# 64-row tile products, val by blocks one group earlier, tangent features on VectorE, and a new order, in a cosformer and SwiGLU kernel

## The chip, the cores and the metric

The kernel runs on one core of a Trainium2 chip. A core has TensorE (PE: matrix products, with weight loads that overlap them), VectorE (DVE), ScalarE (ACT), GpSimd (POOL) and SyncE (SP); POOL and SP issue most of the DMAs. Work data lie in SBUF, products land in the eight banks of PSUM. The metric is the time of one execution on the device in microseconds (us), the median over runs.

## The reference

Two layers behind one another: an attention without softmax, linear in the sequence, and a gated feed-forward block.

```python
batch, n_heads, seq, head_dim = (8, 8, 576, 64)
theta = np.pi / 2.0 * np.arange(S) / S
def phi(x, c, s):                       # c, s: cos and sin of theta
    r = np.maximum(x, 0.0)
    return np.concatenate([r * c, r * s], axis=-1)
q_p, k_p = phi(q, cos_w, sin_w), phi(k, cos_w, sin_w)
kv = np.einsum('bhsf,bhsd->bhfd', k_p, v)
z = np.sum(k_p, axis=2)
num = np.einsum('bhsf,bhfd->bhsd', q_p, kv)
den = np.einsum('bhsf,bhf->bhs', q_p, z)[..., None] + 1e-06
x = (num / den).transpose(0, 2, 1, 3).reshape(B * S, H * D)      # 4608 x 512
g, val = x @ w_gate, x @ w_val                                   # 512 x 1536 each
out = (g * (1.0 / (1.0 + np.exp(-g))) * val) @ w_out             # 1536 x 512
```

The kernel divides the features by the cosine: a query row then has the features relu(q) and relu(q) times its tangent.

## The kernel before, in words

**Tiles and groups.** The 4608 tokens are 36 tiles of 128, four tiles to a group, nine groups (0 to 8). A tile is two slots of 64 tokens; a batch is nine slots, so tile 4 has a slot of batch 0 and one of batch 1, tiles 5 to 8 lie in batch 1, and so on.

**Attention.** For each batch the key sums `kv` and `z` come from `kv_job` (line 716): 64-row, 64-column products in the four quarters of PE's array. For batches from 2 on the query features are written to `r_q` (`feature_jobs`): relu by VectorE in two instructions, and nine instructions that multiply a slot by its tangent and take the relu, on ScalarE (line 877; batch 7 does both kinds on ScalarE, line 867). A DMA transpose on SP's queue turns them to `phit` (line 839). A tile's products with the key sums are in `tile_jobs`: line 785 for tiles of batches from 2 on, line 779 for tiles 4 to 8. The latter multiply 128 rows, two heads one above the other, with a block-diagonal matrix (`kvd`, `kvd1`) of 130 columns: eight products a tile, sixteen in tile 4. Then come the denominator (line 797), its reciprocal (line 803), the product with it into `x` (line 807), and the turn of `x` to `xT`: by PE for tiles 4 to 7 (line 755), by a DMA transpose on SP's queue from tile 8 on (line 747).

**Feed-forward.** A group has twelve slices of 128 hidden columns, in three units u = 0, 1, 2 of four slices. Gate and val of a unit can be taken in two ways. Plain: four slices of four products of 512 columns each (`plain_fc`, line 904, or `plain_val`, line 1052). By blocks (`block_jobs`, line 977): seven products of sums instead of eight, each of four matmuls of 256 columns; VectorE makes sums of `xT` (line 950), of the weights (line 499), and two adds for each unit between the products (lines 997 and 1005 or 1013), ScalarE copies two products (line 628). `GATE_FROM` and `VAL_FROM` say from which (group, unit) on blocks are used: gate from (1, 0), val from (2, 1). The multiplication of silu(gate) with val is line 1061 (plain) or line 1072 (blocks). The output projection is plain in group 0 (line 1262) and by blocks from group 1 on (line 1142), behind token sums by VectorE (line 1093).

**Loads.** `batch_loads` puts a `hold_job` ahead of loads on GpSimd's queue: a tiny copy that reads a given tile, so that what is queued behind it starts only when that tile is there. Batch 3's k and v and batch 4's q are held by tile 8's `xT`.

**The order.** The first quarter of group 0 follows a list written out by hand (`words`). Everything behind it is a set of `Job`s, each with engines, a duration, what it comes after, and rooms (banks, buffers) it takes and gives back; `order_once` plays them through on these costs and due times, shaken by a list of `SEEDS`, one for each `WINDOW` of planned time, and the instructions are emitted by planned start.

Of the kernel before, what the change touches and what calls it, by code (L numbers as in the profile page):

```python
# [19 lines left out]
def kernel(  # L20
# [10 lines left out]
    nc = tc.nc  # L31
# [374 lines left out]

    xT = {}
# [175 lines left out]
    TAIL = {"PE": 206.0, "ACT": 160.0, "DVE": 140.0, "POOL": 150.0, "SP": 150.0}  # L583
    PAD = 12.0
# [19 lines left out]
    def sc(n, sbuf=False):  # L604
        return 69 + n / 1.2 + (27 if sbuf else 0) + PAD

# [29 lines left out]
    def relu_on(eng, out, in_):  # L636
# [11 lines left out]
    LOADED = {("k", 1): 440.0, ("v0", 1): 7580.0, ("v1", 1): 9080.0, ("sa", 1): 10080.0, ("sb", 1): 14480.0, ("q", 2): 22280.0,  # L648
              ("k", 2): 25580.0, ("v", 2): 29580.0, ("q", 3): 32380.0}
    WO_AT = ((0, 2, 11330.0), (2, 4, 12580.0), (4, 8, 16980.0), (8, 12, 19480.0))  # L650
    W_AT = {8: (1750.0, 3060.0), 10: (4820.0, 6130.0)}
# [19 lines left out]
    DEN_ON = {"ACT": 100}  # L671
# [35 lines left out]
    def kv_job(b, key, after):  # L707
# [12 lines left out]
        mm = pe(1404, fn, key, after=after, get=[r], chore=b > 1)  # L720
        outs = []
        for n in range(2):
            for i in range(2):
# [8 lines left out]
                outs.append(Job({"ACT": 402, "DVE": 450} if b == 1 else {"ACT": 402}, fn, after=[mm] + J_.get(("tiles", b - 2), []), put=[r]))  # L732
# [11 lines left out]
    def turn_job(t, x, after, by_pe=False, key=None):  # L744
        if not by_pe:
            def fn(j):
                nc.sync.dma_start_transpose(out=xT_of(t), in_=one(x_all, x))
            J_["xT", t] = Job({"SP": 1450}, fn, after=after + J_.get(("xT_read", t // OUT - 3), []), put=[x], tail=X_LAND, dma=(1430.0, X_SVC))
# [7 lines left out]
        mm = pe(230, fn, key, after=after, get=[r], put=[x])  # L756
# [5 lines left out]
    X_LAND = 4000.0  # L762
    X_SVC = 1030.0
    PHI_LAND = 11500.0

    def tile_jobs(t, key, by_pe=False):
# [3 lines left out]
        def fn(j):  # L770
            ps = bank(r)
            for e in range(2):
                for g in range(G):
                    for ms, b, c, n in parts_of(t):
                        if b < 2:
                            if g % 2:
                                continue
                            for w in range(2):
                                nc.tensor.matmul(  # L779
                                    out=ps[ms, e, g * D1:(g + 2) * D1],  # L780
                                    lhsT=late[:, 2 * (t % 2) + w, e, g // 2].rearrange("p c s -> p (c s)")[:, ms],
                                    rhs=(kvd1 if b else kvd)[:, e, g // 2, w].rearrange("p i x -> p (i x)"),
                                    start=w == 0, stop=w == 1)
                            continue
# [4 lines left out]
        mm = pe(690 if 0 in bs else 455 if 1 in bs else 520 if len(bs) == 2 else 262, fn, key, after=sum((J_["kv", b] + turned_for(b, t) for b in bs), []), get=[r, one_at], chore=not by_pe)  # L789

        def view():
            return bank(r)[:, :, 0:2 * J * D1].rearrange("p e (y x) -> p e y x", x=D1)

        def fn(j):
            o, i_ = den_all[:, t % 4].rearrange("p (e y) o -> p e y o", e=2), view()[:, :, :, D:D1]
# [8 lines left out]
        rec = Job({"DVE": 132}, fn, after=[den])  # L804

        def fn(j):
            tt(out=one(x_all, x).rearrange("p (y e d) -> p e y d", e=2, d=D), in0=view()[:, :, :, 0:D],  # L807
               in1=rec_all[:, t % 4].rearrange("p (e y) o -> p e y o", e=2).to_broadcast([P, 2, 4, D]), op=ALU.mult)
# [8 lines left out]
    def load_job(b, nm, after, lands, behind):  # L817
        def fn(j):
            (load_turned if nm == "q" else load)(b, nm)
        J_["load", b, nm] = Job({"POOL": 1600 if nm == "q" else 780}, fn, after=after, tail=lands, behind=behind, dma=(1940.0, 2460.0) if nm == "q" else (470.0, 3770.0))  # L820

    def hold_job(read, after, put=()):
        def fn(j):
            nc.gpsimd.tensor_copy(out=hold2, in_=read())
        jb = Job({"POOL": 480}, fn, after=after, put=put)
# [3 lines left out]
    def batch_jobs(b, key):  # L829
# [11 lines left out]
        turned = [Job({"SP": 7500}, fn, after=phis + J_.get(("tiles", b - 2), []), tail=PHI_LAND - 7500, dma=(7600.0, 1370.0))]  # L841
# [10 lines left out]
    def feature_jobs(b):  # L852
# [10 lines left out]
        if b in PHI_ACT:  # L863
            for c in range(NC):
                for w in range(2):
# [3 lines left out]
                    phis.append(Job({"ACT": 412}, fn, after=loaded_q + before + J_["tanq"], rel=landed))  # L869
        else:  # L870
# [4 lines left out]
            for c in range(NC):  # L875
                def fn(j, c=c):
                    nc.scalar.activation(out=home()[:, :, c, 1], in_=raws[b, "q"][:, :, c], func=AF.Relu,  # L877
                                         scale=tanq[:, c:c + 1])
                phis.append(Job({"ACT": 430}, fn, after=loaded_q + before + J_["tanq"], rel=landed))
# [81 lines left out]
    def block_jobs(tg, u, which, order):  # L961
# [10 lines left out]
        def product(r, a, x, first, key, after, **kw):  # L972
# [6 lines left out]
            return pe(437.6, fn, key, after=after, **kw)  # L979
# [125 lines left out]
    def store_jobs(t, after, put, queues, cols=slice(0, d_model)):  # L1105
        for e in range(2):
# [6 lines left out]
            Job({q_: 560}, fn, after=after, put=put, tail=6500.0, dma=(1270.0, 480.0))  # L1113
# [9 lines left out]
    def out_jobs(tg, key):  # L1123
# [10 lines left out]
        def product(n, rs, a, b, first, after, get=(), parts=((range(HC), (0, 1)),), keys=()):  # L1134

            res = []
            for m, (kcs, its) in enumerate(parts):
# [7 lines left out]
                res.append(pe(len(kcs) * len(its) * 109.4, fn, at, after=after(kcs, its), behind=res, get=get if not m else ()))  # L1145
# [151 lines left out]
    def turned_tiles(ts, key):  # L1297
# [14 lines left out]
        mm = pe(200 + 236 * len(ts), fn, key, after=[], get=[r], rel=LOADED["sa" if ts[-1] < 6 else "sb", 1])  # L1312
# [57 lines left out]
    VAL_FROM = (2, 1)  # L1370
# [309 lines left out]
```

## Time and profile before

| | us |
|---|---|
| median of three runs | 298.43 |
| lowest, highest | 298.17, 299.18 |
| the profiled execution, first to last instruction (span) | 296.4 |
| busy: PE, VectorE, ScalarE, GpSimd | 291.1, 252.0, 199.4, 69.6 |

The profile is of one execution; its own time is known as the span, and what lies around the span is in the runs' times alone. PE's clock was granted in full from the first slice to the last. Line numbers are those of the kernel before. In the views that follow, a group reads: line, engine, operation, what is written from what, shapes, count, then busy us, mean ns of one, idle us just ahead, and what ended that idle time.

### The profile page before, as it was taken

To read this page: it belongs to the slowest core of one execution; us is meant where nothing else is said; L and a number is where in the kernel's file an instruction comes from. 1 tells how busy PE (TensorE), PEld (TensorE's weight loads), DVE (VectorE), ACT (ScalarE), POOL (GpSimd) and SP (SyncE) were. 2 spreads that over 40 slices of the span, in tenths; PEclk is the share of its full clock that TensorE was granted. 3 is DMA by queue.
4 is the path that set the end of the run, shared out by engine and by line. 5 is a ranking of instruction groups with operands and counts; after the bars stand their busy time and mean duration, and the time that the engine had idled before them with its cause. 6 is when DMAs were issued, how large, how long until landed. Compare 5 with 4: busy or idle time off the path is not lost.

```text
span 296.4 us, 8073 instructions
## 1 busy us (share of the span) xinstructions
PE 291.1 (98%) x3244; PEld 238.7 (81%) x3244; DVE 252.0 (85%) x514; ACT 199.4 (67%) x421; POOL 69.6 (23%) x122
## 2 busy tenths in 40 slices
PE   8999999999999999999999999999999999999994
PEld 4597465776787888898898889888988888888883
DVE  7878997879877999999988987998679868986883
ACT  6564346989559968985699589967465556565630
POOL 7963630003007012221352023200220050002000
PEclk9999999999999999999999999999999999999999
DMA  7999999997989997799996979940470046002026
GB/s 266 225 196 198 202 206 207 203 205 121 194 177 144 229 190 122 151 171 149 174 203 133 186 113 162 183 81 2 107 110 2 0 97 119 2 0 73 0 58 157
DMA packets 71973, 40.89 MB, mean 138 GB/s; under 512 B 48768, under 2 KB 68736, under 8 KB 71936
## 3 DMA queue, kind: packets, MB, share of 16 engines
q0 software_dynamic: 24800, 24.39, 49.1%
q1 hardware_dynamic: 46528, 15.47, 28.9%
q10 hardware_dynamic: 608, 0.52, 0.7%
q8 instruction: 25, 0.41, 0.6%
q14 instruction: 12, 0.10, 0.1%
HBM read 37.75 MB, written 9.44 MB: 159 GB/s over the span
## 4 chain that ended last, share of the span: by engine, by line
PE 97%; DVE 1%; issue 0%
PE banks L977 45%; PE banks L1142 24%; PE banks L1052 5%; PE banks L1262 4%; PE banks L438 4%; PE banks L904 4%; PE banks L187 3%; PE banks L716 3%; PE banks L785 2%; PE banks L779 1%; PE banks L372 1%; PE banks L1310 0%; PE banks L315 0%; PE banks L418 0%; PE banks L351 0%
## 5 line engine op out<-in xcount | busy, mean ns | idle before, releaser
L1111 POOL DMA_DIRECT2D out_dram<-ob x52 | 27.3, 532 | 104.8 <-ACT ob L630 69.7
L1036 ACT ACTIVATE sg<-banks 128x512 bf16<-128x512 f32 x72 | 41.3, 599 | 5.6 <-PE banks L977 5.4
L977 PEld LDWEIGHTS <-wg_sb 128*128 128x128 f16 x384 | 36.9, 98 | 6.3
L628 ACT COPY banks<-banks 128x512 f32<-128x512 f32 (+1 forms) x53 | 29.9, 572 | 17.5 <-PE banks L977 7.3
L1142 PEld LDWEIGHTS <-ht 128*128 128x128 f16 x384 | 37.4, 98 | 4.8
L1072 DVE TENSOR_TENSOR ht<-sg,banks 128x512 f16<-128x512 bf16 x60 | 39.9, 680 | 0.9 <-PE banks L977 0.6
L977 PEld LDWEIGHTS <-wgs_sb 128*128 128x128 f16 x368 | 35.7, 98 | 4.6
L997 DVE TENSOR_TENSOR banks<-m,banks 128x512 f32<-128x512 f32 x44 | 30.2, 693 | 10.6 <-ACT m L628 8.1
L977 PEld LDWEIGHTS <-wv_sb 128*128 128x128 f16 x320 | 31.0, 98 | 3.8
L977 PE MATMUL banks<-kvt,wgs_sb 128*128 128x256 f16 x236 | 33.4, 273 | 0.0
L1142 PEld LDWEIGHTS <-sums 128*128 128x128 f16 x288 | 27.9, 98 | 3.3
L630 ACT ACTIVATE ob<-banks 128x512 f32<-128x512 f32 x32 | 18.8, 596 | 15.9 <-PE banks L1142 15.2
L977 PE MATMUL banks<-xT,wg_sb 128*128 128x256 f16 x192 | 28.8, 273 | 0.0
L628 ACT COPY m<-banks 128x512 f32<-128x512 f32 x44 | 25.5, 590 | 4.4 <-PE banks L977 4.3
L1142 PE MATMUL banks<-wo_sb,ht 128*128 128x256 f16 x192 | 25.7, 273 | 0.0
L1142 PE MATMUL banks<-wt_sb,sums 128*128 128x256 f16 x192 | 24.9, 273 | 0.0
L977 PE MATMUL banks<-xT,wv_sb 128*128 128x256 f16 x160 | 24.0, 273 | 0.0
L1036 ACT ACTIVATE sg<-m 128x512 bf16<-128x512 f32 x24 | 15.1, 630 | 12.4 <-DVE m L1005 12.2
L807 DVE TENSOR_TENSOR x<-banks,rec 128x512 f16<-128x512 f32 x32 | 21.6, 686 | 1.5 <-DVE rec L803 0.2
L977 PE MATMUL banks<-kvt,wg_sb 128*128 128x256 f16 x168 | 22.4, 273 | 0.0
L1142 PE MATMUL banks<-wt_sb,ht 128*128 128x256 f16 x192 | 22.3, 273 | 0.0
L877 ACT ACTIVATE r_q<-raw_q,tanq 128x256 bf16<-128x256 bf16 x45 | 20.7, 510 | 0.1
(160 smaller groups left out, 544.7 us busy)
## 6 DMA issues: line engine op xcount, KB each, us to landing
out_dram<-ob POOLq DMA_DIRECT2D x52, 128.0 KB, 3.9
raw_kv<-in_k_dram POOLq DMA_DIRECT2D x7, 576.0 KB, 5.9
raw_q<-in_q_dram POOLq DMA_DIRECT2D x12, 288.0 KB, 10.7
raw_kv<-in_v_dram POOLq DMA_DIRECT2D x6, 576.0 KB, 8.3
out_dram<-ob SPq DMA_DIRECT2D x12, 128.0 KB, 2.5
wg_sb<-in_moe_w_gate_dram POOLq DMA_DIRECT2D x5, 256.0 KB, 8.9
wv_sb<-in_moe_w_val_dram POOLq DMA_DIRECT2D x5, 256.0 KB, 9.5
wo_sb<-in_v_dram SPq DMA_DIRECT2D x2, 576.0 KB, 4.2
```

The source lines that it names most:

```text
L438: nc.tensor.matmul(out=st["f", tg, fc, lo][i], lhsT=(wg_sb, wv_sb)[i][:, kc, fs], rhs=xT[tg][:, ts, kc], start=(kc == 0), stop=(kc == KC - 1))
L628: nc.scalar.copy(out=out, in_=in_)
L630: nc.scalar.mul(out=out, in_=in_, mul=mul)
L807: tt(out=one(x_all, x).rearrange("p (y e d) -> p e y d", e=2, d=D), in0=view()[:, :, :, 0:D], in1=rec_all[:, t % 4].rearrange("p (e y) o - ...
L877: nc.scalar.activation(out=home()[:, :, c, 1], in_=raws[b, "q"][:, :, c], func=AF.Relu, scale=tanq[:, c:c + 1])
L977: nc.tensor.matmul(out=to[:, i], lhsT=a[:, c, 2 * u + i], rhs=x()[:, :, c], start=first and i == 0 and c == 0, stop=c == KH - 1, skip_grou ...
L997: tt(out=bank(c), in0=one(m7_all, m).rearrange("p i x -> p (i x)"), in1=bank(b), op=ALU.add)
L1036: nc.scalar.activation(out=gates(rooms[w])[:, :, jh * HT:(jh + 1) * HT], in_=src, func=AF.Silu, scale=DOWN)
L1052: nc.tensor.matmul(out=bank(v), lhsT=wv_sb[:, kc, fc * P:(fc + 1) * P], rhs=xT[tg][:, :, kc], start=(kc == 0), stop=(kc == KC - 1))
L1072: tt(out=ht[:, 4 * u + w:4 * u + w + 3:2, jh * HT:(jh + 1) * HT], in0=gates(rooms[w])[:, :, jh * HT:(jh + 1) * HT], in1=src.rearrange("p ( ...
L1111: {"POOL": nc.gpsimd, "SP": nc.sync, "ACT": nc.scalar}[j.eng].dma_start(out=out_v[idx // NC, idx % NC][:, cols], in_=ob_of(t)[e * SH:(e + ...
L1142: nc.tensor.matmul(out=to, lhsT=a[:, kc, i * P:(i + 1) * P], rhs=b[:, kc], start=first and kc == 0 and i == 0, stop=kc == HC - 1, skip_gro ...
```

## The change

Five things, and with them the whole order of the jobs behind the hand-written list.

```diff
 tile_jobs, tiles of batches 0 and 1
-                            if g % 2:
-                                continue
                             for w in range(2):
-                                nc.tensor.matmul(
-                                    out=ps[ms, e, g * D1:(g + 2) * D1],
-                                    lhsT=late[:, 2 * (t % 2) + w, e, g // 2].rearrange("p c s -> p (c s)")[:, ms],
-                                    rhs=(kvd1 if b else kvd)[:, e, g // 2, w].rearrange("p i x -> p (i x)"),
-                                    start=w == 0, stop=w == 1)
+                                for i in range(0 if g % 2 else 2):
+                                    rows = slice(i * D, (i + 1) * D)
+                                    nc.tensor.matmul(
+                                        out=ps[ms, i, (g + e) * D1:(g + e + 1) * D1],
+                                        lhsT=late[rows, 2 * (t % 2) + w, e, g // 2].rearrange("p c s -> p (c s)")[:, ms],
+                                        rhs=(kvd1 if b else kvd)[rows, e, g // 2, w, i], start=w == 0, stop=w == 1)
...
-        mm = pe(690 if 0 in bs else 455 if 1 in bs else 520 if len(bs) == 2 else 262, fn, key, ...)
+        mm = pe(386 if 0 in bs else 352 if 1 in bs else 387 if len(bs) == 2 else 259, fn, key, ...)
...
+            x_, rec_ = one(x_all, x), heads(rec_all[:, t % 4])
+            if pairs and not by_pe:
+                for jj in range(J):
+                    ys = slice(2 * jj, 2 * jj + 2)
+                    tt(out=x_.rearrange("p (j i e d) -> p j i e d", i=2, e=2, d=D)[:, jj], in0=view()[:, :, ys, 0:D],
+                       in1=rec_[:, :, ys].to_broadcast([P, 2, 2, D]), op=ALU.mult)
+                return
 turn_job, by PE
-                nc.tensor.transpose(out=ps[:, kc], in_=one(x_all, x)[:, kc * P:(kc + 1) * P], identity=ident16)
+                nc.tensor.transpose(out=ps[:, kc], in_=one(x_all, x)[:, by_pairs(kc) * P:(by_pairs(kc) + 1) * P], identity=ident16)
 feature_jobs, batches 2 to 6
-                    nc.scalar.activation(out=home()[:, :, c, 1], in_=raws[b, "q"][:, :, c], func=AF.Relu,
-                                         scale=tanq[:, c:c + 1])
-                phis.append(Job({"ACT": 430}, fn, after=loaded_q + before + J_["tanq"], rel=landed))
+                    nc.vector.tensor_scalar(out=home()[:, :, c, 1], in0=raws[b, "q"][:, :, c], scalar1=tanq[:, c:c + 1],
+                                            scalar2=0.0, op0=ALU.mult, op1=ALU.max)
+                phis.append(Job({"DVE": 197}, fn, after=loaded_q + before + J_["tanq"], rel=landed))
 val by blocks
-    VAL_FROM = (2, 1)
+    VAL_FROM = (1, 0)
 batch 3's loads
-            if b == 3:
-                batch_loads(lambda: xT[2][0:1, 0, 0, 0:2], [J_["xT", 8]], names)
-            else:
+            if b > 3:
                 batch_loads(phit_read, J_["turned", b - 1], names)
         for t, s in tiles:
             tile_jobs(t, (tg, s / 4))
+            if t == 11:
+                batch_loads(lambda: xT[2][0:1, 3, 0, 0:2], [J_["xT", 11]], names)
 the planner's costs and the order
-    PAD = 12.0
+    PAD = 1.0
...
-        mm = pe(1404, fn, key, after=after, get=[r], chore=b > 1)
+        mm = pe(1178, fn, key, after=after, get=[r], chore=b > 1)
...
-    BUSY_AT = {"PE": 0.0, "ACT": 0.0, "DVE": 750.0, "POOL": 0.0, "SP": 0.0}
+    BUSY_AT = {"PE": 1050.0, "ACT": 0.0, "DVE": 1600.0, "POOL": 0.0, "SP": 0.0}
...
-    WINDOW = 10000.0
+    WINDOW = 5000.0
```

In tiles 4 to 8 a product of 128 rows and 130 columns becomes two of 64 rows and 65 columns, one for each head of the pair, which skip the zero blocks and write to two banks; in tile 4 each covers 64 tokens. The bank of a head replaces the bank of e, so the heads' columns come in another order, which `by_pairs` undoes in the PE transposes and a split multiplication undoes in tile 8. The units (1,0), (1,1), (1,2) and (2,0) take val by blocks. Many of the planner's durations, landing times and due times get other values, the shake comes from an own hash instead of Python's generator, and `SEEDS` is another, longer list.

More of the change, by code (lines that the diff above doesn't have):

```diff
@@ L582 @@
     jobs = []
-    TAIL = {"PE": 206.0, "ACT": 160.0, "DVE": 140.0, "POOL": 150.0, "SP": 150.0}
-    PAD = 12.0
+    TAIL = {"PE": 202.0, "ACT": 150.0, "DVE": 128.0, "POOL": 150.0, "SP": 150.0}
+    PAD = 1.0
     def d1(n):
@@ L868, in fn @@
                                              scale=tanq[:, c:c + 1] if w else 1.0)
-                    phis.append(Job({"ACT": 412}, fn, after=loaded_q + before + J_["tanq"], rel=landed))
+                    phis.append(Job({"ACT": 400 if w else 308}, fn, after=loaded_q + before + J_["tanq"], rel=landed))
         else:
```

69 lines of the change are left out of this document (39 added, 30 removed).

## The prediction

> **What bounds the kernel now.** I read the page's busy times first, then the chain of work that ended last, then that chain in order of time.
>
> ```profile
> span 296.4 us, 8073 instructions
> PE 291.1 (98%) x3244; PEld 238.7 (81%) x3244; DVE 252.0 (85%) x514; ACT 199.4 (67%) x421; POOL 69.6 (23%) x122
> PE 97%; DVE 1%; issue 0%
> ```
>
> TensorE (PE) is busy for 291.1 us of 296.4 and holds 97% of the chain. What it is not busy is the first microsecond and the tail behind its last product: the last piece of the chain is VectorE's, at 292.32, and the stores follow it. So a nanosecond taken from PE's work is a nanosecond of the end, as long as no other engine keeps PE waiting; and the three timed runs' median, 298.43, stands 2.0 above the profiled span (298.43 - 296.4), which I carry over.
>
> Busy shares of PE are modelled, so I price PE by the chain in order of time (start, length, line, count), where each piece ends at the start of the next.
>
> ```profile
> 41.47 1.17 PE banks L779 x24
> ...
> 45.26 0.47 PE banks L779 x8
> ...
> 45.95 0.47 PE banks L779 x8
> ...
> 54.66 0.47 PE banks L779 x8
> ...
> 61.22 0.86 PE banks L1052 x4
> 62.09 1.18 PE banks L716 x63
> 63.26 0.97 PE banks L1052 x4
> ...
> 75.42 1.73 PE banks L1052 x8
> ...
> 95.08 0.38 PE banks L785 x16
> 95.46 0.98 PE banks L1052 x4
> ...
> 97.57 9.17 PE banks L977 x84
> ...
> 151.88 15.72 PE banks L977 x144
> ...
> 292.32 0.42 DVE r_q L634
> ```
>
> A product of 512 columns (L1052) takes 1.73 / 8 = 0.216, one of 256 (L977) 15.72 / 144 = 0.109, both at the full rate that neighbouring pieces show. The pieces stand end to end: there is next to nothing but work to gain from.
>
> **Val by blocks.** The four units (1,0), (1,1), (1,2) and (2,0) change from plain val to seven block products. The groups by line and shape price both forms:
>
> ```profile
> L997 DVE TENSOR_TENSOR banks<-m,banks 128x512 f32<-128x512 f32 x44 | 30.2, 693 | 10.6 <-ACT m L628 8.1 <-PE banks L977 1.8 <-ACT sg L1036 0.3
> L628 ACT COPY banks<-banks 128x512 f32<-128x512 f32 x51 | 29.2, 580 | 15.0 <-PE banks L977 7.3 <-PE banks L1142 6.5 <-ACT ob L630 0.7
> L628 ACT COPY m<-banks 128x512 f32<-128x512 f32 x44 | 25.5, 590 | 4.4 <-PE banks L977 4.3
> L1052 PE MATMUL banks<-xT,wv_sb 128*128 128x512 f16 x64 | 16.1, 379 | 0.0
> L1072 DVE TENSOR_TENSOR ht<-sg,banks 128x512 f16<-128x512 bf16 x60 | 39.9, 680 | 0.9 <-PE banks L977 0.6
> L1013 DVE TENSOR_TENSOR sg<-m,banks 128x512 f16<-128x512 f32 x20 | 13.6, 681 | 1.6 <-PE banks L977 1.6
> L1061 DVE TENSOR_TENSOR ht<-sg,banks 128x512 f16<-128x512 bf16 x16 | 10.7, 682 | 1.5 <-PE banks L1052 0.9 <-ACT sg L1036 0.4
> L1072 DVE TENSOR_TENSOR ht<-sg 128x512 f16<-128x512 bf16 x20 | 8.3, 416 | 0.0
> ```
>
> All 64 products of L1052 go: 64 x 0.216 = 13.84 us. In come 4 x 28 = 112 products of 256 columns: 112 x 0.1092 = 12.23. **PE: -1.61 us.** The price is paid elsewhere. Each unit gives up four L1061 (2.73 us) and takes one L997, one L1013, three long L1072 and a short one (0.693 + 0.681 + 3 x 0.680 + 0.416 = 3.83): VectorE +1.10 a unit, 4.4 in all. ScalarE takes two copies a unit, 4 x (0.580 + 0.590) = 4.7. The four x sums that the products read are made for the gates already. The V weight sums exist too; only the last kind moves:
>
> ```profile
> L499 DVE TENSOR_TENSOR wv_sb<-wv_sb x3: 415/417/419, 73.8 to 99.3; 128x512 f16<-128x512 f16 x3
> ```
>
> These three of 0.42 overwrite weights that the plain vals of groups 1 and 2 read, so they run from 73.8 on. Now only group 0's vals must be past, and they are wanted before group 1's M5. 1.25 us more for VectorE before about 60; I cost it at nothing on PE, because the work that PE has from the first tile at 41.47 to the last at 54.66 covers it; without that cover it is at most 0.42 for each unit.
>
> **64-row pairs.** Tiles 4 to 8 take 1.17 + 3 x 0.47 = 2.58 us now; by its share of 24 products tile 4 alone is 1.17 - 0.47 = 0.70. Afterwards tiles 5 to 8 make 16 products each of 64 rows and 65 columns, two of them on different rows of the array, and tile 4 makes 32 quarter products. No row shows pairs by rows. Pairs by columns of the same width and count are in the chain: the tile at 95.08 takes 0.38 for its 16, and the next four products of L1052 take 0.98 instead of 0.86, so leaving a split array costs about 0.11 (0.97 against 0.86 behind L716 as well). Quarter products: L716 issues 72 in 1.18, 0.0164 each, so 32 are 0.52. By these nearest rows: 4 x (0.38 + 0.11) + 0.52 + 0.11 = 2.59, no gain. The ends: if four products of 65 columns at once cost half of L716's 0.0164 each, and a pair no more than that, five tiles are 96 x 0.0082 = 0.79, a gain of 1.8; if pairs don't overlap at all, each product is half of the 0.059 that one of twice its width takes (0.47 / 8), and with a switch on either side the tiles are 96 x 0.0294 + 10 x 0.11 = 3.92, a loss of 1.3. The changed planner's own costs are 0.352 and 0.386, and its cost for L716, 1.178, is the row's 1.18, which speaks for them as times of this chip; with 0.11 for each exit they make 4 x 0.46 + 0.50 = 2.34. **I take -0.3**, between the rows' 0 and those costs without the exit (2.58 - 1.79 = 0.8), nearer to the first.
>
> The Trainium skill, TensorEngine Tiling (Array Packing), section Key Properties, says that changing the tiling mode drains TensorE, which speaks against short bursts such as these. The 0.11 behind L716 and L785 agrees with it. By that rule with a drain on either side the five tiles come to 3.1 and the change to -1.1, 297.3, inside the forecast's own range; by the rows' one-sided 0.11 it is what stands above.
>
> Tile 8's multiplication becomes two of half the width: below 0.2 us on VectorE, beside products. The order of columns in the PE transposes costs nothing, the count of them stays.
>
> **Tangent features.** 45 ScalarE instructions become VectorE's.
>
> ```profile
> L877 ACT ACTIVATE r_q<-raw_q,tanq 128x256 bf16<-128x256 bf16 x45 | 20.7, 510 | 0.1
> L283 DVE TENSOR_SCALAR r_q<-raw_q 128x1152 bf16<-128x1152 bf16 x10 | 4.2, 457 | 0.6 <-DMA raw_q<-in_q_dram 0.6
> L283 DVE TENSOR_SCALAR raw_kv<-ht 128x256 bf16<-128x256 f32 x1 | 0.3, 274 | 0.0
> 71.98 1.28 DVE L1061 TENSOR_TENSOR ht<-sg,banks 128x512 f16<-128x512 bf16 x2
> ```
>
> ScalarE loses 20.7. On VectorE the nearest row is the 256-column one, 274 ns; in a row each instruction hides about 0.08 of the next (two of 682 take 1.28), so 0.19 each. Bounds: 0.10 (457 x 256 / 1152, no fixed part) and 0.42 (a PSUM form of that width is no faster than the 416 above). I take 45 x 0.19 = 8.6 us; per batch 1.7. None of it is on PE; what hides it is VectorE's idle time:
>
> ```profile
> 54.20:65.00 10.80, 10.80 (x150) 7.97 (x148) 9.14 (x18) 9.95 (x22) 0.00 (x0) 1.00 1.18 224
> 65.00:77.15 12.15, 12.15 (x99) 7.90 (x98) 11.49 (x23) 9.86 (x23) 2.90 (x5) 1.00 0.79 129
> 77.15:97.60 20.45, 20.45 (x262) 16.47 (x261) 15.83 (x34) 15.22 (x35) 5.51 (x10) 1.00 1.02 173
> 97.60:117.00 19.40, 19.40 (x180) 17.27 (x179) 18.43 (x35) 15.51 (x31) 4.00 (x7) 1.00 1.00 174
> 117.00:136.00 19.00, 19.00 (x260) 16.96 (x258) 18.23 (x35) 16.35 (x37) 4.21 (x8) 1.00 0.96 168
> ```
>
> (Stretch, its length, then busy time of PE, weight loads, VectorE, ScalarE, GpSimd.) From 54.2 to 136 VectorE is busy 73.1 of 81.8. Added there: 4.4 and three batches of features, 5.1: 82.6, in a stretch that becomes 79.9. That looks like too much, but busy time counts the 0.08 of each of the 145 instructions that stands alone; packed closely the same work needs up to 11 us less, 71 to 83. I cost it at nothing, with the rival below as the price if that cover fails.
>
> **Batch 3's loads.** The hold and its three loads (four DMAs on GpSimd's queue: k, v, and q in two) wait for tile 11's turn instead of tile 8's.
>
> ```profile
> 66.19 6.76 SPq L747 DMA_TRANSPOSE xT<-x  x4
> 68.69 0.17 POOL L824 CAST hold<-xT 1x2 bf16<-1x2 f16 x1 [27.14 <-DMA xT<-x]
> 88.24 0.17 POOL L824 COPY hold<-phit 1x2 bf16<-1x2 bf16 x1 [16.18 <-DMA phit<-r_q]
> 84.00 0.76 DVE L950 TENSOR_TENSOR kvt<-xT 128x512 f16<-128x512 f16 x2 [1.45 <-DMA xT<-x]
> 106.88 0.75 DVE L950 TENSOR_TENSOR kvt<-xT 128x512 f16<-128x512 f16 x2
> ```
>
> Now the loads go out while the transposes of tiles 9 to 11 are still under way, and the last of these lands at 84.0, 11 us after its issue, with VectorE's x sums waiting. Without the loads beside them the turns should land some microseconds earlier; the loads start between 73 and 84 instead of at 69. Behind the hold on its queue stands only the next hold, at 88.24, after 16 us of idle; SP's queue keeps its order. What is late next is batch 3's key sums, its tiles (95.08 is one) and through their turns the x sums of group 3, now at 106.88. Meanwhile PE has group 2's block products (9.17 from 97.57) and then its output products, seven times twelve, 84 x 0.109 = 9.2. With the loads 4 to 8 us later, less what they gain by not sharing the engines with the turns, this covers it, and I take nothing; with the full 15 (84 against 69) the x sums would come at 122, past that work (97.6 + 9.2 + 9.2 = 116), and PE could lose up to 6.
>
> **The sum.** -1.61 - 0.3 = -1.9: span 294.5, time 296.5. The whole order is new, though, and the only clear wait in the middle of PE's work,
>
> ```profile
> 241.79 0.33 PEld L977 LDWEIGHTS <-vsums 128*128 128x128 f16 x4 [0.24 <-DVE x L807]
> ```
>
> may go or come back elsewhere: 0.24 either way, taken as nothing.
>
> **The rivals.** (1) VectorE becomes the bound from 54 to 136. For it: 95% and 96% busy already from 97.6 to 136. At that 96%, 82.6 needs 86.0, 6.1 more than 79.9. Against it: the 0.08 overlaps, and weights and token sums that can slip. It decides where the adds behind block products (L997, L1013) come so late that no filled bank is left for PE. With half the 6.1 paid: 299.5, slower. (2) The seven-product chain, with its copy and two adds between products, makes PE wait about 0.4 a unit where plain vals ran freely, and the gain is eaten: 298.2, no change. Against it: units (2,1) on already run so, in pieces like the 144 products at 151.88 without a gap. (3) The pairs run at twice the rate and without switches, 0.79 and an exit for each tile, 1.34 in all, -1.2 instead of -0.3: 295.6. (4) Batch 3's loads come the full 15 us late and PE loses half of the 6: 299.5 too.
>
> **How the numbers follow.** 0.61 for 296.5 (its own range 295.9 to 297.4), 0.13 for 295.6, 0.14 for 298.2, 0.12 for the two at 299.5 (0.09 and 0.03). A time more than 0.3% (0.9 us) off is what a measurement can tell from no change: faster below 297.5, slower above 299.3. Faster 0.75 (the first two and the near edge of the third), same 0.13, slower 0.12. The range 295.4 to 298.9 leaves out most of the slow case and a little below (3).
>
> **What would show it.** L1052 is gone and L977 has 112 more products at 0.109; tiles 4 to 8 sum to 2.3 on the chain; L877 is VectorE's at 0.19 to 0.27 and VectorE's busy time is near 265, ScalarE's near 183; the hold stands past 73 and the x sums of group 2 no longer wait for a transpose. I am wrong if PE shows waits for VectorE between 54 and 136 that add to over 1 us, or if the end moves without PE's work having shrunk.

## The result and the profile after

| | before | after |
|---|---|---|
| median of four runs each, us | 298.30 | 307.74 |
| lowest, highest | 298.09, 299.18 | 306.21, 308.68 |
| profiled execution (span) | 296.4 | 306.9 |

The changed kernel is slower: after over before is 1.0306, 95% interval 1.0274 to 1.0338. The profiled execution of after is the slowest of its four (308.68). Here and below, an execution over 1.5% above the fastest of its kernel counts as slow and is left out of medians and ranges. From the page of after:

```profile
span 306.9 us, 8293 instructions
PE 292.4 (95%) x3340; PEld 243.4 (79%) x3340; DVE 260.6 (85%) x568; ACT 187.3 (61%) x384; POOL 69.5 (23%) x122
PEclk9999999999999987999999999999999999999999
PE 78%; DMA 11%; DVE 5%; ACT 1%; issue 1%; POOL 1%; DVEq 0%; SPq 0%; ACTq 0%
```

Before, PE held 97% of the chain. Now transfers hold 11% and VectorE 5%, and the granted clock dips once. The wait view of PE says for what PE stood (us in total, times, longest). Before, its only entry was 1.0 us at the very start.

```profile
PE banks L990 <- ACT sg L1049: 5.8, 1, 5.8
PE banks L990 <- DVE kvt L963: 1.5, 1, 1.5
PE banks L990 <- DVE x L820: 1.2, 2, 1.0
PE banks L990 <- DMA xT<-x: 1.1, 1, 1.1
```

These are 9.6 us. The engines named waited too. Three groups, first of before and then of after, with the idle time ahead of them and what ended it behind the last bar:

```profile
L281 ACT ACTIVATE raw_kv<-raw_kv 128x576 bf16<-128x576 bf16 (+1 forms) x25 | 16.4, 707 | 1.1 <-DMA raw_kv<-in_k_dram 1.1
L950 DVE TENSOR_TENSOR kvt<-xT 128x512 f16<-128x512 f16 x14 | 5.5, 416 | 2.0 <-DMA xT<-x 1.4 <-PE banks L977 0.5
L807 DVE TENSOR_TENSOR x<-banks,rec 128x512 f16<-128x512 f32 x32 | 21.6, 686 | 1.5 <-DVE rec L803 0.2
```

```profile
L280 ACT ACTIVATE raw_kv<-raw_kv 128x576 bf16<-128x576 bf16 (+1 forms) x25 | 16.4, 706 | 8.3 <-DMA raw_kv<-in_k_dram 8.3
L963 DVE TENSOR_TENSOR kvt<-xT 128x512 f16<-128x512 f16 x14 | 5.5, 418 | 8.5 <-DMA xT<-x 8.2
L820 DVE TENSOR_TENSOR x<-banks,rec 128x512 f16<-128x512 f32 x31 | 21.0, 684 | 4.1 <-DMA xT<-x 3.1
```

The same work, at the same mean, waits 19.6 us for transfers (8.3 + 8.2 + 3.1) where it waited 2.5 (1.1 + 1.4). An engine takes its queue in order, so what stands behind such an instruction waits too. The timeline at the largest of these places:

```profile
97.56 2.50 POOL L1124 DMA_DIRECT2D out_dram<-ob  x4 [16.73 <-ACT banks L630]
100.17 2.08 POOL L1124 DMA_DIRECT2D out_dram<-ob  x4
102.23 0.80 POOL L120 DMA_DIRECT2D raw_kv<-in_k_dram  x1
103.02 0.78 POOL L120 DMA_DIRECT2D raw_kv<-in_v_dram  x1
114.47 1.25 ACT L280 ACTIVATE raw_kv<-raw_kv 128x576 bf16<-128x576 bf16 x2 [7.63 <-DMA raw_kv<-in_k_dram]
116.26 1.01 PE L990 MATMUL banks<-xT,wv_sb 128*128 128x256 f16 x4 [5.79 <-ACT sg L1049]
117.07 1.06 PE L1155 MATMUL banks<-wo_sb,ht 128*128 128x256 f16 x4
118.12 0.76 DVE L963 TENSOR_TENSOR kvt<-xT 128x512 f16<-128x512 f16 x2 [6.55 <-DMA xT<-x]
119.63 0.62 PE L990 MATMUL banks<-xT,wv_sb 128*128 128x256 f16 x4
```

Batch 4's keys are asked for at 102.23, behind eight output stores, and land at 114.4. Their relus stand at the head of ScalarE's queue for 7.63 us; a silu (L1049) stands behind them, and PE waits 5.79 us for it. In the same stretch two turns of x are issued, and VectorE stands 6.55 us at the x sums that need them. The tile view of xT for turns issued from 103 to 106:

```profile
DMA to landing us min/median/max: 12.7/13.3/14.0
```

After the wait PE is slow for a while: the four products at 117.07 take 1.06 us where the four at 119.63 take 0.62; from start to start it is 0.21 each instead of 0.109. The stretches (length, PE, weight loads, VectorE, ScalarE, GpSimd, granted clock, transfers, GB/s) show the clock:

```profile
106.00:110.00 4.00, 4.00 (x39) 3.59 (x38) 4.00 (x8) 0.84 (x2) 0.00 (x0) 1.00 1.83 140
110.00:116.00 6.00, 0.47 (x5) 0.28 (x3) 1.57 (x5) 1.53 (x3) 0.00 (x0) 0.74 0.87 127
116.00:120.00 4.00, 3.74 (x20) 2.65 (x20) 1.84 (x6) 3.56 (x8) 1.67 (x3) 0.54 0.09 12
```

The Trainium skill, TensorE: Matmul & The Clock Gate, Part 1, says that an idle array is throttled to half rate until it has been busy for some 3.4 us; the 0.54 in the four microseconds behind the wait agrees. About 16 products are hit, 1.6 us at (0.21 - 0.109) each, from the 3.37 us between 116.26 and the next full-rate piece at 119.63.

And PE's own work did shrink. Tiles 4 to 8 (L784) in its chain in order of time, with the warm-up products ahead of everything and the x sums of group 2:

```profile
0.99 7.74 PE banks L186 x56
...
41.90 0.39 PE banks L784 x32
...
44.26 0.60 PE banks L784 x32
44.85 0.97 PE banks L1275 x4
...
46.04 0.86 PE banks L1275 x4
...
47.13 0.35 PE banks L784 x16
...
67.34 0.35 PE banks L784 x16
...
77.48 4.03 DMA xT<-x
81.61 0.77 DVE kvt L963 x2
```

They sum to 1.69 us (2.58 before), but leaving the split array costs again: the four products at 44.85 take 0.97 where those at 46.04 take 0.86. With 0.11 for each of three such exits (behind 44.26, 47.13 and 67.34) the tiles come to 2.0, 0.6 less than before. L1052 is gone for 112 products. The warm-up products are the same in the chain of before, but took less there:

```profile
0.99 6.88 PE banks L187 x56
```

The span's +10.5 is then: waits 9.6, slow products 1.6, work -0.6 (tiles with their exits) and -1.6 (val by blocks, by its count and the rate of 0.109), 0.9 at the start (7.74 - 6.88), and 0.6 in small pieces that I don't put down to anything. The 0.9 is not the change's: the same products take 7.67 in one profile of the old parts (s_bseed, below) and 6.97 in one of the new (f6_loads_early).

### The profile page after: what moved, and what is told of

It reads as the page before. It is cut to its first block, busy times and chain, and to the rows that moved or that the text cites. A ratio compares the mean times of both kernels' runs of the same rounds, so it can differ in the third digit from the quotient of the medians.

```text
span 306.9 us, 8293 instructions
## 1 busy us (share of the span) xinstructions
PE 292.4 (95%) x3340; PEld 243.4 (79%) x3340; DVE 260.6 (85%) x568; ACT 187.3 (61%) x384; POOL 69.5 (23%) x122
## 4 chain that ended last, share of the span: by engine, by line
PE 78%; DMA 11%; DVE 5%; ACT 1%; issue 1%; POOL 1%; DVEq 0%; SPq 0%; ACTq 0%
PE banks L990 37%; PE banks L1155 21%; DMA xT<-x 7%; DMA raw_kv<-in_k_dram 4%; PE banks L1275 4%; PE banks L440 3%; PE banks L917 3%; PE banks L186 3%; PE banks L718 2%; DVE x L820 2%; DVE ht L1085 1%; POOL out_dram L1124 1%; PE banks L789 1%; PE banks L371 1%; DVE m L1018 1%
## 5 line engine op out<-in xcount | busy, mean ns | idle before, releaser
L1085 DVE TENSOR_TENSOR ht<-sg,banks 128x512 f16<-128x512 bf16 x72 | 48.2, 677 | 1.5 <-ACT banks L630 1.2
L990 PEld LDWEIGHTS <-wv_sb 128*128 128x128 f16 x384 | 37.1, 98 | 11.0 <-issue 6.1
L1049 ACT ACTIVATE sg<-banks 128x512 bf16<-128x512 f32 x72 | 41.2, 597 | 5.5 <-PE banks L990 5.5
L630 ACT COPY banks<-banks 128x512 f32<-128x512 f32 (+1 forms) x57 | 31.6, 571 | 19.2 <-PE banks L990 11.8
L1010 DVE TENSOR_TENSOR banks<-m,banks 128x512 f32<-128x512 f32 x48 | 32.9, 690 | 12.2 <-PE banks L990 9.4
L990 PEld LDWEIGHTS <-wgs_sb 128*128 128x128 f16 x384 | 37.1, 98 | 6.6 <-issue 2.0
L990 PE MATMUL banks<-kvt,wgs_sb 128*128 128x256 f16 x252 | 36.3, 273 | 1.7 <-DVE kvt L963 1.5
L990 PE MATMUL banks<-xT,wv_sb 128*128 128x256 f16 x192 | 29.2, 276 | 5.8 <-ACT sg L1049 5.8
L630 ACT COPY m<-banks 128x512 f32<-128x512 f32 x48 | 28.1, 592 | 6.2 <-PE banks L990 5.8
L820 DVE TENSOR_TENSOR x<-banks,rec 128x512 f16<-128x512 f32 x31 | 21.0, 684 | 4.1 <-DMA xT<-x 3.1
L1049 ACT ACTIVATE sg<-m 128x512 bf16<-128x512 f32 x24 | 15.1, 630 | 14.7 <-DVE m L1018 11.3
L990 PE MATMUL banks<-kvt,wv_sb 128*128 128x256 f16 x168 | 23.3, 273 | 0.0
```

The costliest lines, as they stand in the source:

```text
L630: nc.scalar.copy(out=out, in_=in_)
L820: tt(out=x_.rearrange("p (i y d) -> p i y d" if pairs else "p (y e d) -> p e y d", d=D, **({"i": 2} if pairs else {"e": 2})), in0=view()[: ...
L990: nc.tensor.matmul(out=to[:, i], lhsT=a[:, c, 2 * u + i], rhs=x()[:, :, c], start=first and i == 0 and c == 0, stop=c == KH - 1, skip_grou ...
L1010: tt(out=bank(c), in0=one(m7_all, m).rearrange("p i x -> p (i x)"), in1=bank(b), op=ALU.add)
L1049: nc.scalar.activation(out=gates(rooms[w])[:, :, jh * HT:(jh + 1) * HT], in_=src, func=AF.Silu, scale=DOWN)
L1085: tt(out=ht[:, 4 * u + w:4 * u + w + 3:2, jh * HT:(jh + 1) * HT], in0=gates(rooms[w])[:, :, jh * HT:(jh + 1) * HT], in1=src.rearrange("p ( ...
```

## The experiments

My theory after this reading, called the order theory in the expectations: the parts of the change are worth about what was forecast, and the new order loses 9 us because instructions that need a transfer stand at the head of in-order queues before it has landed; I blamed the planner, whose figures for landing are much shorter after the change. Rivals: VectorE is filled, the chain of seven products or the pairs cost by themselves, batch 3's later loads cost by themselves.

**One place of the order moved.** Two kernels with after's instructions, each with one group of jobs at another place of its queue.

```diff
 f1_krelu_late
+    at_ = {j: j.start + 9000.0 for j in jobs if J_["load", 4, "k"] in j.after}
 f2_loads_first
+    loads = [J_["load", 4, "k"], J_["load", 4, "v"]]
...
+    at_ = {j: first - 10.0 + n for n, j in enumerate(loads[0].after[:1] + loads)}
 both
-    for j in sorted(jobs, key=lambda j: j.start):
+    for j in sorted(jobs, key=lambda j: at_.get(j, j.start)):
```

> The kernel after with one edit of its order: the four relus of batch 4's k stand 9 us of planned time further back in ScalarE's queue; every instruction and every other place is kept. In the profile of the kernel after they stand at the head of that queue from 106.8 to 114.5 us, waiting for k, and the silu that TensorE waits 5.8 us for stands behind them. Order theory (queues in order, planned on transfers that land later than their figures): the 5.8 us wait for the silu goes, but VectorE's sums of x still wait for a turn until 118 us, so TensorE loses 1 to 4 us there; the time is 302 to 306. Rival, one of the four parts of the change costs the time by itself (VectorE full, the seven-product chain, the pairs): the place of four relus decides nothing, 306 to 309.

306.06 (304.74 to 306.42), 1.0238 of before. The wait view of the run:

```profile
PE banks L990 <- DVE kvt L963: 5.8, 2, 4.3
```

ScalarE's wait is gone, and the next queue takes its place: PE waits 4.3 us for VectorE's x sums. Only 1.7 us are won. The time lies where my range ends and the rival's begins, so the run does not part them; the wait that goes and the one that comes are what it shows.

> The kernel after with one edit of its order: on GpSimd's queue batch 4's hold and its loads of k and v stand ahead of group 1's output stores instead of behind them. Order theory: the loads are issued about 4 us sooner (102.2 before), k lands sooner by as much, so the wait of 5.8 us at 110 us shrinks to 1 to 3 us, while the turns of x beside the loads land at best as before; 302 to 306. If the landing is late because the stores and the loads share the transfer engines whatever their order, nothing is won: 306 to 309. Rival, a part of the change costs the time by itself: 306 to 309 too.

309.76, slower than after and outside both ranges. Transfers issued from 97 to 105 in this run (count, size, median us to landing):

```profile
raw_kv<-in_k_dram POOLq DMA_DIRECT2D x1, 576.0 KB, 6.6
...
xT<-x SPq DMA_TRANSPOSE x3, 9.0
```

The keys land 10 us sooner than in after, but the turns beside them still take 9.0, and PE waits 6.4 us for VectorE, which is held by a turn. So in this run the late thing that matters is the turns, not the keys.

**Other orders.** The planner's figures for transfers, with tie-breaking numbers (`SEEDS`) searched anew, and in two kernels those numbers alone.

```diff
 s_land: transfers' costs and landing times of before in after, SEEDS searched anew
-    X_LAND = 400.0
+    X_LAND = 4000.0
-    PHI_LAND = 1300.0
+    PHI_LAND = 11500.0
...
 s_ctrl: after, s_bseed: before, only SEEDS other
```

> All four parts of the change kept (pairs, blocks, features on VectorE, batch 3's loads behind tile 11's turn) and the new costs of the computing instructions, but the planner has the transfers' costs and landing times of before again (a turn of x 5.45 us, the turn of phi 11.5, loads 7.3 to 9.3, stores 7), and the tie-breaking numbers are searched anew for that; the planned end is 270.7 us against 265.4 of after and 269.7 of before. Order theory: no wait of over 2 us for ScalarE's or VectorE's queue at 100 to 120 us is left; 296 to 300. Rivals: VectorE full or the chain and pairs on TensorE, or batch 3's later loads, cost the 9 us whatever the order: 303 to 309.

319.18 (315.1 to 319.39): the worst of all, and outside both ranges. The planned end is 5.3 later than after's, less than half of the 11.4 that it loses against after. My blame of the short figures is not borne out. Transfers issued from 105 to 110 in this run:

```profile
raw_q<-in_q_dram POOLq DMA_DIRECT2D x2, 288.0 KB, 17.7
out_dram<-ob POOLq DMA_DIRECT2D x4, 128.0 KB, 12.0
xT<-x SPq DMA_TRANSPOSE x1, 2.4
phit<-r_q SPq DMA_TRANSPOSE x1, 19.9
```

A turn of phi beside four stores and two loads of queries takes 19.9 us; no fixed figure, 8.5 or 11.5, stands for that. What a transfer takes depends on what is beside it: the turn of x ahead of them took 2.4.

> The kernel after, planner's figures and all, with other tie-breaking numbers found from nothing (planned end 269.3 us, 3.9 later than after's and 1.4 sooner than the order with the old transfer figures): another order made with the same short transfer times. Order theory: the short times spoil this order too, though the waits fall in other places; 303 to 312. If after's own order was only unlucky in one spot, this one has no wait of over 3 us: 298 to 302, no slower than the order with the old transfer figures by more than 2.

309.57 (308.84 to 312.86), as the theory had it: another order of the same parts loses too, in other places (turns at 108 and 176 to 180). A cause in the parts would say the same.

> The kernel before, all its parts and its planner's figures, with other tie-breaking numbers found from nothing (planned end 272.8 us against 269.7): an order of the old kernel that was never tried on a chip. Order theory: an order not tried on the chip loses several us to transfers whatever the kernel's parts, so 303 to 315, with waits of TensorE behind ScalarE's or VectorE's queue that a transfer holds. Rival, after's parts are the cause: the old parts lose only what the plan says, 300 to 302.

302.93, between the two expectations: 4.2 above before's 298.72 in the same runs, of which the planned end has 3.1. PE's longest wait in it, but for the 1.0 at the start, is for the V weight sums:

```profile
PE banks L977 <- DVE wv_sb L499: 1.1, 1, 1.1
```

Another order of the old kernel loses 1.1 more than its plan says, not 10 us, and the three groups above wait some 0.6 us for transfers in it, against 7.8 in s_ctrl. So a new order is not enough by itself; the new parts, or the planner's new figures, have to do with it.

**Parts put into the old order.** Pairs, and pairs with features on VectorE, with the planner's costs of before kept, so that each instruction keeps its place.

```diff
 g_pairs, g_pairs_feat: tile_jobs of after, costs of before
 g_pairs_feat
-                    nc.scalar.activation(out=home()[:, :, c, 1], ...
+                    nc.vector.tensor_scalar(out=home()[:, :, c, 1], ...
                 phis.append(Job({"ACT": 430}, ...
```

> The kernel before with two of the parts (64-row pairs in tiles 4 to 8, tangent features on VectorE), every instruction at its old place in the order. Order theory: 297 to 299. Rival, VectorE full: 300 or more, with waits of TensorE for VectorE between 54 and 136 us that before does not have. Rival, pairs dearer than 128 rows: the matmuls of tiles 4 to 8 sum to over 2.6 us and the time is 299 to 300.

> The kernel before with one part of the change, the 64-row pairs in tiles 4 to 8, every instruction at its old place in the order. In the run with pairs and features the pairs' matmuls sum to 1.8 us where the old form took 2.6, so by the pairs alone the time falls by 0.5 to 1: 297.2 to 298.2 against 298.5. Rival, the 6 us of that run come from the pairs' side (the multiplications in two halves, the other order of x): 300 to 305; else they come from the features on VectorE.

304.86 with both, 299.94 with the pairs alone (12 executions, 298.3 to 302.5), ratio 1.0045 (1.0015 to 1.0074). Waits with the pairs alone, then with both:

```profile
PE banks L991 <- DMA xT<-x: 2.0, 1, 2.0
```

```profile
PE banks L991 <- DMA xT<-x: 1.9, 1, 1.9
PE banks L785 <- DVE phit L1340: 1.2, 1, 1.2
```

Both runs missed what I expected; the time with both is the one that the rival "VectorE full" gave. The pairs' products take 1.79 us instead of 2.58, and PE then meets a wait of 2.0 for a turn that before doesn't have, in the profiled execution; the times scatter over 4 us where before's scatter over 2. The features cost 5 us more in an order that was made for ScalarE: VectorE's later work makes a turn and the last features of the early tiles late. A run with these two parts and batch 3's later loads (g_three, 307.35) took that batch's key sums before its moved work was done, and settles nothing.

**Parts taken out of after.** Features back on ScalarE, and batch 3's loads behind tile 8's turn, each with all other places kept.

> The kernel after with one part undone: the 45 tangent features run on ScalarE again, each at its place in after's order. Rival, VectorE is filled by the features: VectorE falls to about 252 us busy, its waits go, 300 to 304. Order theory: the wait at 110 us (ScalarE's queue held by the load of k) stays as it is, 306 to 310.

> The kernel after with one part undone: batch 3's loads wait for tile 8's turn again, as in before, instead of tile 11's, about 4 us sooner; all other places are kept. Rival, the later loads of batch 3 are what costs, by all that follows from them: 300 to 304. Order theory: the turns of tiles 9 to 11 land later beside the loads, the wait at 80 us grows from 1.7 to 3 to 6 us and the one at 110 stays: 307 to 312.

314.08 and 315.61, outside both ranges. Each part undone alone costs 6 to 8 us more. That does not show the parts to be free in after: the order was written for them, and with the features back ScalarE has 16 us more to do (203.3 busy instead of 187.3) at places planned for VectorE. Waits of the first, then of the second:

```profile
PE banks L990 <- ACT banks L630: 4.6, 5, 1.7
...
PE banks L990 <- ACT sg L1049: 1.8, 1, 1.8
```

```profile
PE banks L990 <- DVE kvt L963: 7.5, 1, 7.5
PE banks L990 <- ACT sg L1049: 4.0, 1, 4.0
```

With the earlier loads the wait for group 2's x sums grows from 1.5 to 7.5: waiting for tile 11's turn was right in this order. With the features on ScalarE PE waits five times for that engine's copies. I had expected the long wait for batch 4's keys to stay in both; it is 1.8 and 4.0.

**The loads behind the turns.** The hold ahead of a batch's loads reads the turn of another tile, and the relus and weightings of that batch stand later by as much.

```diff
+            nc.gpsimd.tensor_copy(out=hold2, in_=xT[t // 4][0:1, t % 4, 0, 0:2])
...
+        for n, j in enumerate([hold] + mine):
+            at_[j] = J_["xT", t].start + 10.0 + n
...
 batch, tile: f3_b4 (4, 15); f3_turns_first (4, 15), (6, 23); f7_more (4, 15), (6, 20); f8_b3 (3, 10), (4, 15), (6, 20)
```

> The kernel after with its order edited at two places: batch 4's loads of k and v wait for the turn of tile 15 and batch 6's for that of tile 23 (before, for the turn of phi, which comes sooner), and the relus and weightings that read them stand as much later in ScalarE's and VectorE's queues; all other places are kept. Order theory: the turns at 103 to 106 us land 2.4 to 5 us after their issue instead of 12.7 to 14, the 5.8 us wait and the slow products behind it go, and most of the 1.1 us wait at 173; no wait of TensorE over 2.5 us is left; 297 to 302. Rival, a part of the change costs the time by itself: the waits move elsewhere and the time is 304 to 309.

> The kernel after with its order edited at one place: batch 4's loads of k and v wait for the turn of tile 15, and the relus and weightings that read them stand as much later; batch 6 is left as in after. Order theory: the wait at 110 us stays gone as in the run with both edits, and the 5.9 us wait at 174 us that came with batch 6's edit is 1 to 2 us again: 301.5 to 305. Rival, a part of the change costs the time wherever the waits fall: 306 to 310.

Batch 4 alone: 302.78 (302.62 to 303.64), 5.0 of the 9.4 us back from one edit, where the relus alone had brought 1.7 (f1_krelu_late). Transfers issued from 101.5 to 110 and the timeline:

```profile
raw_kv<-in_k_dram POOLq DMA_DIRECT2D x1, 576.0 KB, 5.8
...
xT<-x SPq DMA_TRANSPOSE x2, 3.9
```

```profile
108.82 0.79 POOL L120 DMA_DIRECT2D raw_kv<-in_k_dram  x1
114.77 2.39 ACT L280 ACTIVATE raw_kv<-raw_kv 128x576 bf16<-128x576 bf16 x4
```

The turns land after 3.9 us instead of 13.3. And the keys, asked for 6.6 us later than in after, are there at the same moment: the relus start at 114.77 against 114.47. Against this run, asking early in after won nothing for the load and cost the turns 9 us. With batch 6 edited as well (310.3) the time is lost again, by a wait of 5.7 us at 174.

> The kernel after with batch 4's loads behind tile 15's turn as before, and two places more edited in its order: batch 6's loads of k and v wait for tile 20's turn (the relus and weightings that read them stand later by as much), and the second four output stores of group 4 stand behind the four turns of that group. The run with batch 4 alone still had waits of TensorE of 1.4 us at 167, 1.6 at 193 and 1.5 at 121 to 124. Order theory, transfers that are issued just ahead of a turn and what queues behind them: the first two go, 298.5 to 301. Rival, the 4 us that were left over before belong to the parts of the change: the time stays at 301.5 to 304 and the waits move.

> As the run with the two places more, and batch 3's loads wait for tile 10's turn too, which the change leaves behind its hold (the wait of 1.7 us at 80 us). Order theory: that wait shrinks below 0.4 us, and TensorE may wait up to 1 us for batch 3's key sums at 91 us in its place; 297 to 300.5, 0.5 to 1.5 below the run without it. Rival: the transfers behind collide anew and it is slower than the run without it by 1 us or more.

306.29 and 310.92: the rivals of both were nearer. Batch 6's loads, moved out of the turns' way, fall on the turn of phi (18.0 us to landing in the first run), and batch 3's make its key sums late by 2.8. The output stores of the first were meant to stand behind the four turns, issued from 155.8 to 162.7, and one still went out at 158.9: a later place in GpSimd's queue did not hold it back, since nothing made it wait for SyncE's. No edit of mine beats the kernel before.

**The loads taken away.** To tell waits from the price of the parts, the loads of keys and values of batches 3 to 7 are left out of three kernels, and queries' loads of one.

```diff
-            (load_turned if nm == "q" else load)(b, nm)
+            if nm == "q":
+                load_turned(b, nm)
+            else:
+                raw_of(b, nm)
```

> The kernel before without the loads of keys and values of batches 3 to 7 (10 loads of 576 KB; the work on them runs on what earlier batches left in the same buffers); order, instructions and everything else are kept. Its TensorE has no wait over 0.3 us for a transfer already, so the time stays at 296.5 to 298.7 by every theory; it is the one that the next is held against.

> The kernel after without the same 10 loads of keys and values of batches 3 to 7; everything else is kept. Order theory, the 9.4 us are waits for transfers beside those loads and what queues behind them: the waits at 80, 110, 173 and 200 us go or fall below 0.5 us, and what is left is TensorE's smaller work: 293.5 to 297.5, that is 1 to 3 us less than the kernel before without them. Rival, the parts cost by themselves (VectorE filled by the features, the chain of seven products): it stays 3 to 9 us above the kernel before without them, 300 to 307.

> The kernel before with pairs and features at the old places (304.9 with all loads), without the same 10 loads of keys and values of batches 3 to 7. If its 6 us are waits for transfers too: 296 to 299. Rival, VectorE pays for the features wherever the transfers land: 301 to 305, with TensorE's waits for VectorE as in the run with the loads.

> The kernel after without the loads of keys and values of batches 3 to 7 and without the loads of queries of batches 4 to 7 as well (features of all of them run on batch 3's queries); everything else is kept. The run without keys and values left 301.05, with TensorE's waits of 1.4, 1.7, 1.1 and 0.6 us at 80, 105, 192 and 251 us, beside turns that land 3 to 6 us after their issue. If those turns are late for the queries' loads, the waits shrink below 0.5 us each and the time is 297 to 299.5. If they are late for the output stores and for what stands in the order, the time stays at 300 to 301.5.

| | time, us | over before |
|---|---|---|
| before, without k and v | 298.40 | 0.9989 (0.9979 to 1.0000) |
| after, without k and v | 301.05 | 1.0078 (1.0063 to 1.0093) |
| after, without k, v and q | 299.72 | 1.0033 (1.0019 to 1.0047) |
| pairs and features in before's order, without k and v | 303.08 | 1.0143 (1.0124 to 1.0161) |

Before doesn't notice whether the loads are there; after loses 6.7 us of its 9.4 with them, and 1.3 more with the queries'. Instructions and order are the same in each pair; only what is on the way to SBUF, and what waits for it, differs. So most of the loss is waiting that these loads bring. It does not reach the 293.5 to 297.5 that I expected: 301.05 lies in the rival's 300 to 307, though 2.7 above before without the loads and not 3 to 9, and 299.72 lies between the two ranges of its run. What PE still waits for, without k and v and then without q too:

```profile
PE banks L993 <- DVE x L820: 2.9, 3, 1.6
PE banks L993 <- DVE kvt L966: 1.2, 1, 1.2
```

```profile
PE banks L993 <- DVE x L820: 3.1, 3, 1.8
```

L820 is the product into `x`, and most of its idle time in these runs is a wait for an earlier turn that has yet to free a buffer of `x` (3.7 and 3.9 us), now beside the output stores. Take the 3.1 from 299.72 and 296.6 is left; that is a sum and not a run, since no order without these waits was found. The fourth kernel keeps 4.7 of its 6 us without the loads: as its rival said, there the features on VectorE do cost, in an order made for ScalarE.

## Why the prediction was wrong

**The step that failed** is the last term of the sum, that the order is new but may be "0.24 either way, taken as nothing". It measured 9.6 us of waits and 1.6 of slow products behind them. The prediction's own sign of being wrong came with it: PE waits 1.5 us for VectorE at 81, inside 54 to 136, and 5.8 for ScalarE from 110. The profile of before has no wait to speak of, and I carried that over. It does not mean that its transfers are quick: its slowest turn of x takes 12.2 us, after's 14.0. What differs is how long instructions at the head of a queue stand for a transfer, 2.5 us before and 19.6 after, and what PE has to do meanwhile.

That most of the waits come with the loads is shown (6.7 of 9.4 us go without those of keys and values). Why after has them and before has not is open: the three orders of the new parts lose 9 to 21 us (after, s_ctrl, s_land), another order of the old parts only 1.1 more than planned. Either the new parts leave less room for a late transfer in any order, or the planner's new costs do; no run keeps the one and changes the other.

**Val by blocks**: right as far as shown. L1052 is gone, PE has 112 block products instead, and the waits that the chain was suspected of (rival 2) aren't there: none of the four waits of after is for the adds L1010 and L1018. No run changes this part alone, so its -1.61 was not measured by itself.

**64-row pairs**: right. In the run with the pairs alone, every place kept, the stretch from the first of these products to the sixteen behind tile 8 takes 15.0 us (41.80 to 56.81) instead of 15.4 (41.47 to 56.88): -0.4, and -0.6 in after, for a forecast of -0.3. With their exits the tiles come to 2.0 to 2.2, near the 2.34 by the planner's costs with exits; rival 3 (1.34, -1.2) was further off. The 3.1 by the rule of the Trainium skill (TensorEngine Tiling (Array Packing), Key Properties) is further off than that 2.34: the pieces just ahead of these tiles are no longer than others, and the 0.11 is seen behind them alone.

**Tangent features**: VectorE's busy time is 260.6, not near 265, ScalarE's 187.3 for 183. The features are 7.6 of VectorE's 8.6 more (253.0 with them back on ScalarE), near the forecast's 8.6, and the rest, 1.0, is all that is left of the 4.4 that val by blocks was to add there; off ScalarE they take 16.0, not 20.7. Whether the cover held in after's own order stays open. For it: at the waits inside 54 to 136 VectorE itself waits for a transfer (1.69 us at 81, 6.55 at 118). Against it: ahead of the wait at 174 the chain of after runs through 1.2 us of the moved features to a product into `x`, and then through that tile's turn of 9.0. In before's order the cover did not hold, 5 us. So rival 1 had the right place, the stretch from 54 to 136; that VectorE's amount of work is the cause is not shown.

**Batch 3's loads**: the hold stands at 77.46, inside 73 to 84. That "the x sums of group 2 no longer wait for a transpose" was wrong: the new order puts tile 10's turn behind the hold, where its 4.03 us beside the loads cost 1.5 of PE's time. What I called "late next", group 3's x sums, lies in the stretch where the largest wait arose, though not by batch 3's loads: batch 4's keys and values were asked for in front of tile 14's and 15's turns.

**The rivals** all had their price on one engine's work or on batch 3. None had the mechanism that the runs point to: a load beside a turn, and queues that stop at what the two bring.

**What stays open**: whether the new parts or the order make the waits; why batch 4's keys took 12.2 us in after where 5.7 to 6.9 is usual, beyond the eight stores and two turns that were on the way with them; and whether an order exists in which all parts together reach 296.5.

## What to carry to other kernels

When an edit makes a scheduler write a new order for a kernel that waits for nothing, the order may be the largest unknown, as it was here: find, for each in-order queue, the first instruction that needs a transfer, what stands behind it, and what else is on the way when that transfer is issued. Try asking for a large load behind the small urgent transfers, not in front of them: batch 4's keys landed at the same moment, and the turns 9 us sooner. It is no rule: the same edit for batch 6 lost what batch 4's had won. Leaving the loads out of both kernels tells in one pair of runs how much of a loss is waiting for them or beside them.

## What was not expected of the hardware

- A turn of x takes 2.4 us alone, 3.9 beside stores, 12.7 to 14.0 beside stores and 1.15 MB of loads, and a turn of phi 7.2 to 19.9, over all profiles here. The Trainium skill, DMA: Bandwidth & Descriptors, Rules for kernel authors, says that transfers from different engines run on the same 16 DMA engines and interleave; the turns, on SyncE's queue and late for GpSimd's loads, agree.
- One wait of 5.8 us cost 1.6 more: the clock was granted at 0.54 in the four microseconds behind it.
- The kernel before, without waits, repeats within 2 us (17 executions, 298.1 to 299.9); with the pairs alone, whose one profile has a wait of 2.0 us for a turn, the times scatter over 4 (298.3 to 302.5). That this wait comes and goes is likely, but one profile does not show it.
